# A wait of GpSimd for VectorE's products in a fused recurrence and highway layer, with another list of operations

## The chip, the core and the metric

The kernel runs on one core of a Trainium2 chip. The metric is the device time of one execution in microseconds (us). The engines are named as in the profile: PE is TensorE (PEld its weight loads), DVE is VectorE, ACT is ScalarE, POOL is GpSimd, SP is SyncE, which here issues the transfers. Each engine works through its own queue in order, and they wait for each other by semaphores.

## The reference

Two layers in a row. The first is a gated recurrence over 6,336 steps for 4 sequences of 256 channels, the second a highway layer on its 25,344 outputs:

```
f = lower_bound + (1 - lower_bound) * sigmoid(f_logit)
h = f[:, t] * h + (1 - f[:, t]) * x[:, t]        # for each t; y[:, t] = h
H = max(y @ w_h, 0)
T = sigmoid(y @ w_t + b_t)
out = T * H + (1 - T) * y
```

## The kernel before

The tokens are cut into 29 units, most of 1,024 tokens, the first three and the last three smaller, and one that takes the ends of all four sequences (unit 14). The 256 channels are two halves of 128 partitions. Every unit passes through the same steps, each of which is a small function named by one letter:

- l, x: the loads of f_logit and x, issued by SyncE (w is the store of the output).
- u: on ScalarE, the sigmoid of -f_logit, in f16.
- b: the product of u and x, in pieces of 512 columns, written to bv. Both inputs lie in SBUF. It runs on GpSimd, or on VectorE where the list has a "v" behind it.
- i and p: on TensorE, the transposes of u and of bv, to channels by tokens, into PSUM (tiles uT and bT).
- f: the gate, from uT, on ScalarE (with a "v" on VectorE).
- s: on VectorE, the scan that is the recurrence, from f in SBUF and bT in PSUM, one for each half; it carries the last column on to the next unit.
- z and g: on TensorE, the two matrix products of the highway layer, into PSUM.
- t: on ScalarE, the sigmoid of z.
- d: on VectorE, from y in SBUF and g in PSUM, the maximum and the subtraction of y (the scale 1 - lower_bound is folded into the weights and into the sums).
- E and e: the product of d and t, both in SBUF, which together cover 2 x 1,024 columns of a unit. The last number of each entry of `units` says how many of these columns GpSimd takes, in pieces of 512 (E, with a piece number); VectorE takes the rest in one operation (e). Where the number is 2,048, there is no e; where it is 0, no E.
- o: on TensorE, y times a diagonal plus e, transposed back; c: the copy of the result from PSUM to SBUF, on ScalarE (with "v" on VectorE).

There is no loop over the units: the string `order` lists all these operations one by one, as letter, unit, piece and, behind a colon, the PSUM slot. `pin` keeps the instructions in this order, so the list gives each engine's queue: an engine's queue is the list, cut down to that engine's operations. "e10" is thus VectorE's product of unit 10, and "b15.2" the third bv product of unit 15. Tiles rotate through the numbers of buffers given in `bufs` (6 for l and x, 3 for u and bv, 4 for y, 2 for t, d and e).

The lines in the profile of before: u L233, b L242, i L249, f L264 (VectorE) and L266 (ScalarE), p L280, s L297, z and g L308, t L321, d L326, E and e L332, o L351 and L352, c L360 (VectorE) and L362 (ScalarE).

Of the kernel before, what the change touches and what calls it, by code (L numbers as in the profile page):

```python
# [19 lines left out]
def kernel(  # L20
# [10 lines left out]
    nc = tc.nc  # L31
# [16 lines left out]
        (0, 128, 8, 5120, 'yk', 4, 768),
        (1, 128, 8, 0, 'y', 4, 512),
        (1, 128, 8, 1024, 'y', 4, 2048),  # L50
        (1, 128, 8, 2048, 'y', 4, 1024),
        (1, 128, 8, 3072, 'y', 4, 512),
        (1, 128, 8, 4096, 'y', 4, 0),
        (1, 128, 8, 5120, 'y', 4, 2048),
# [1 line left out]
        (2, 128, 8, 192, 'y', 4, 1024),
        (2, 128, 8, 1216, 'y', 4, 2048),
        (2, 128, 8, 2240, 'y', 4, 768),
        (2, 128, 8, 3264, 'y', 4, 1280),
        (2, 128, 8, 4288, 'y', 4, 2048),  # L60
        (2, 128, 8, 5312, 'y', 4, 1280),
# [1 line left out]
        (3, 128, 8, 1216, 'y', 4, 512),
        (3, 128, 8, 2240, 'y', 4, 2048),
        (3, 128, 8, 3264, 'y', 4, 1024),
        (3, 128, 8, 4288, 'y', 4, 1792),
# [11 lines left out]
c1.0 f4.1 t3.0 s4.0 g3.0:1 i5.0:1 p4.1:0 z3.1:2 d3.0 s4.1 b5.0 b5.2 b5.3 b5.1 f5.0 u6 g3.1:0 t3.1 o2.0:1 E3.0
i5.1:1 p5.0:0 E3.1 d3.1 z4.0:2 s5.0 f5.1 g4.0:0 i6.0:1 p5.1:0 c2.0 u7 t4.0 f6.0 b6.0 d4.0 z4.1:1 g4.1:0 E3.2
b6.2 b6.1 b6.3 s5.1 i6.1:1 e3 d4.1 u8 t4.1 z5.0:2 E4.0 b7.0 p6.0:0 b7.3 t5.0 x8 E4.1 b7.2 f6.1 l10 w0.0 g5.0:0  # L80
l9 z5.1:1 o3.1:2 w2.0 p6.1:1 s6.0 i7.0:0 d5.0 x11 w1.0 b7.1 c3.1 b8.0 x9 b8.2 o3.0:0 b8.1 f7.0 t5.1 c3.0
g5.1:2 s6.1 d5.1 p7.0:0 i8.0:1 e4 f8.0 E5.0 z6.0:1 t6.0 s7.0 E5.1 b8.3 E5.2 x10 g6.0:0 p7.1:1 g6.1:2 i7.1:0
d6.0 z6.1:1 u9 o4.1:0 E5.3 d6.1 o4.0:2 f7.1 u10 b9.0 p8.0:0 c4.0 s7.1 s8.0 i8.1:1 l11 c4.1v t6.1 w3.1 w3.0
z7.0:2 l12 w4.0 f8.1 t7.0 b9.3 b9.1 E6.0 b10.0 x12 g7.0:1 E6.1 i9.0:1 f9.0 i10.1:0 g7.1:2 z7.1:0 b9.2 d7.0
d7.1 f10.1 E6.2 u11 p8.1:1 s8.1 o5.0:1 c5.0 E6.3 o5.1:2 E7.0 c5.1 w5.0 p9.0:0 i9.1:1 t7.1 s9.0 g8.0:1 E7.1
b10.1 d8.0 o6.1:2 p9.1:0 b10.3 l13 w4.1 z8.0:0 w5.1 f9.1 c6.1 i10.0:1 x13 u12 w6.1 l15 b10.2 s9.1 g8.1:1 l14
z8.1:2 e7 p10.0:0 t8.0 d8.1 g9.0:0 t8.1 b11.0 o6.0:2 f10.0 u13 c6.0 d9.0 b11.3 p10.1:1 o7.1:1 z9.0:0 s10.0
c7.1 w6.0 E8.0 b11.1 i11.0:0 g9.1:2 b12.0 z9.1:1 t9.0 s10.1 f11.0 o7.0:0 b12.1 t9.1 d9.1 b11.2 e8 E9.0 w7.1
E9.1 i12.1:1 b12.3 b12.2 p11.0:0 s11.0 f12.1 z10.0:2 c7.0 i11.1:1 g10.0:1 f11.1 x14 d10.0 i12.0:0 p11.1:1
o8.0:0 s11.1 t10.0 w7.0 f12.0 l16 E9.2 c8.0 E9.3 p12.0:0 o8.1:2 u14 x15 s12.0 c8.1 z11.0:1 w8.0 i13.0:1 t11.0  # L90
b13.0 g11.0:0 f13.0 x16 z10.1:2 w8.1 d11.0 p12.1:0 o9.1:1 b13.2 t10.1 b13.1 g11.1:0 l17 b13.3 E10.0 c9.1 w9.1
# [6 lines left out]
p16.0:0 t14.1 i17.1:1 s16.0 o12.1:1 c12.0 x19 f17.1 w12.0 g15.0:2 d14.1 i17.0:0 E13.3 l20 b17.3 c12.1 w12.1
p16.1:1 b18.2 b18.3 d15.0 f17.0 x20 s16.1 z15.0:1 p17.0:0 o13.1:0 u19 o13.0:2 e14 t15.0 E15.0 c13.0 E15.1
i18.0:1 c13.1 s17.0 z15.1:1 z16.0:2 t15.1 t16.0 g15.1:0 d15.1 b19.0 g16.0:1 b18.1 w13.0 d16.0 f18.0 b19.3  # L100
o14.1:2 i19.0:0 p17.1:1 c14.1 f19.0 w13.1 o14.0:0 i18.1:0 l21 u20 b19.2 s17.1 E16.0 b19.1 g16.1:2 d16.1
z16.1:1 p18.0:1 x21 w14.1 l22 z17.0:2 e15 E16.1 f18.1 c14.0 w14.0 x22 b20.0 o15.1:0 p18.1:0 t16.1 t17.0
# [5 lines left out]
p21.0:0 w17.1 z20.1:0 E19.1 u23 c17.0 z20.0:1 p21.1:1 t20.0 b22.3 E19.2 E19.3 w17.0 s21.0 b23.0 b23.3 s21.1
t20.1 x24 o18.0:2 i22.0:0 g20.0:1 l26 g20.1:0 c18.0 d20.0 b23.1 o18.1:2 d20.1 p22.0:1 l25 E20.0 f22.0 u24
o19.1:1 s22.0 z21.0:0 p22.1:0 c18.1 t21.0 g21.0:2 i23.0:1 c19.1 z21.1:0 s22.1 b23.2 E20.1 e20 w18.0 o19.0:1  # L110
f23.0 x25 b24.0 t21.1 E20.2 c19.0 p23.0:1 i23.1:0 d21.0 z22.0:0 g22.0:2 f23.1 s23.0 i24.1:0 t22.0 b24.1 d22.0
E21.0 b24.3 g21.1:1 f24.1 w18.1 x27 d21.1 b24.2 E21.1 u25 z22.1:0 p23.1:1 t22.1 E21.2 x26 i24.0:0 g22.1:2
o20.0:1 s23.1 w19.1 l27 d22.1 o20.1:0 E21.3 b25.0 f24.0 c20.0 b25.1 p24.0:1 i25.1:0 c20.1 s24.0 z23.0:1 u26
b25.3 E22.0 g23.0:2 o21.1:0 d23.0 w19.0 t23.0 p24.1:1 s24.1 f25.1 o21.0:1 w20.0 l28 i25.0:0 E23.0 b25.2
g23.1:2 c21.1 z23.1:0 d23.1 c21.0 x28 w20.1 z24.0:1 e22 p25.0:1 f25.0 u28 t23.1 E23.1 E23.2 t24.0 p25.1:0
z24.1:2 g24.0:0 o22.0:1 t24.1 w21.0 u27 E23.3 s25.0 o22.1:2 d24.0 i26.0:1 c22.0 s25.1 E24.0 f26.0 w21.1
o23.1:0 c22.1 g24.1:1 i26.1:1 b26.0 d24.1 c23.1 i27.0:0 g25.0:2 f27.0 f26.1 z25.0:0 i27.1:0 d25.0 w22.1 w22.0
b26.1 w23.1 p26.0:1 f27.1 z25.1:1 E24.1 e24 b27.0 p26.1:0 s26.0 t25.0 s26.1 b28.0 t25.1 o24.1:2 o23.0:0 c24.1
p27.0:1 s27.0 g25.1:1 c23.0 z26.0:2 i28.1:0 t26.0 o24.0:0 p27.1:1 f28.1 d25.1 E25.0 g26.0:2 e25 s27.1 z26.1:1
w23.0 c24.0 w24.1 d26.0 p28.0:0 E25.1 E25.2 g26.1:0 d26.1 i28.0:1 w24.0 t26.1 e26 z27.0:2 E25.3 t27.0 f28.0  # L120
o25.1:1 g27.0:0 d27.0 o25.0:2 c25.1 z27.1:0 p28.1:1 s28.0 w25.1 o26.0:1 c25.0 g27.1:2 t27.1 s28.1 d27.1
g28.0:0 d28.0 c26.0 e27 z28.0:2 t28.0 g28.1:1 z28.1:0 t28.1 d28.1 e28 o27.0:2 w25.0 c27.0 w26.0 o28.1:1 c28.1
o28.0:0 w27.0 c28.0v w28.1 w28.0
"""

    NU = len(units)
# [109 lines left out]
    def do_b(n, k, eng, slot):  # L236
        np_ = units[n][1]
        if "bv" not in st[n]:
            st[n]["bv"] = sb([P, NB // 2, D, 2], BF16, "bv")
# [2 lines left out]
        pin(e.tensor_mul(st[n]["bv"][:np_, k].rearrange("p d j -> p j d"), st[n]["u"][:np_, q:q + 2],  # L242
                         st[n]["x"][:np_, q:q + 2]))
# [85 lines left out]
    def times(n, eng, a, e):  # L329
        if "e" not in st[n]:  # L330
            st[n]["e"] = flat("e")
        pin(eng.tensor_mul(st[n]["e"][:, a:e], st[n]["d"][:, a:e], st[n]["t"][:, a:e]))  # L332
# [75 lines left out]
```

## Time and profile before

| | us |
|---|---|
| median of 3 runs | 230.56 |
| lowest, highest | 228.42, 241.39 |
| the profiled execution | 228.91 |
| its span | 227.1 |
| DMA: HBM read, written | 52.43 MB, 25.95 MB |

The span goes from the first to the last instruction of the profiled execution. A row of a table of groups gives line, engine and operation, what is written and read with its shape, how often, and then busy time in us, the mean of one in ns, and the idle time of the engine just before them with what ended it. A row of the order of time gives its start in us from the start of the span, how long it took, engine, line and tile, and the count where several were merged; behind it, in brackets, stands idle time before it. A row of waits gives who waited for whom: us in total, how often, and the longest. In a table of stretches each engine has its busy time and, in brackets, its instructions; then come the clock that TensorE was granted (1 is full speed), the share of the DMA engines that was busy, and GB/s.

### The profile page before, as it was taken

The numbers are of one execution on the slowest core, as the hardware profiler recorded it, in microseconds if no ns is written. First come the engines' busy times: TensorE is split into PE (matmuls) and PEld (weight loads), VectorE is DVE, ScalarE is ACT, GpSimd is POOL, SyncE is SP. The second block draws the span as 40 slices with busy tenths as digits, with TensorE's granted clock in tenths as the row PEclk, the third lists the DMA queues.
The fourth block names the chain that finished last, engine by engine and source line by source line (L and its number), as shares of the span: only waits on it lengthen the run. The fifth ranks groups of instructions, "written<-read, shape, count | busy, mean of one in ns | idle before, by whom it ended". The sixth has DMA issues, their size and how long they took to land.

```text
span 227.1 us, 4665 instructions
## 1 busy us (share of the span) xinstructions
PE 189.4 (83%) x1784; PEld 134.3 (59%) x1811; DVE 212.3 (93%) x164; ACT 195.8 (86%) x196; POOL 178.0 (78%) x167
## 2 busy tenths in 40 slices
...
GB/s 187 384 423 421 420 420 418 413 422 421 415 388 318 429 412 419 362 422 428 74 271 382 273 272 416 389 389 351 424 379 331 369 414 266 277 131 270 142 294 223
DMA packets 16751, 78.69 MB, mean 346 GB/s; under 512 B 2004, under 2 KB 2776, under 8 KB 11096
## 3 DMA queue, kind: packets, MB, share of 16 engines
...
q10 hardware_dynamic: 8, 0.00, 0.0%
HBM read 52.43 MB, written 25.95 MB: 345 GB/s over the span
## 4 chain that ended last, share of the span: by engine, by line
PE 31%; DVE 24%; DMA 16%; ACT 11%; POOL 8%; issue 6%; SPq 1%; DVEq 0%; ACTq 0%; POOLq 0%
DMA x<-in_x_dram 10%; DVE y L297 9%; DVE e L332 8%; PE g L308 7%; DMA l<-in_f_logit_dram 7%; PE z L308 6%; DVE d L326 5%; PE op L352 5%; PE op L351 5%; POOL e L332 5%; PE uT L249 4%; ACT f L266 4%; PE bT L280 4%; POOL bv L242 4%; ACT u L233 4%
## 5 line engine op out<-in xcount | busy, mean ns | idle before, releaser
L242 POOL TENSOR_TENSOR bv<-u,x 128x512 bf16<-128x512 f16 x96 | 110.9, 1182 | 14.2 <-ACT u L233 8.7
L297 DVE TENSOR_TENSOR_SCAN y<-f,y,bT 128x1024 bf16<-128x1024 f16 (+2 forms) x46 | 93.1, 2035 | 1.4 <-PE bT L280 1.0
L332 POOL TENSOR_TENSOR e<-d,t 128x512 bf16<-128x512 bf16 (+1 forms) x60 | 68.4, 1153 | 23.5 <-PE op L352 14.7
L321 ACT ACTIVATE t<-z,bt 128x1024 bf16<-128x1024 f32 (+3 forms) x58 | 57.9, 1030 | 13.6 <-DVE e L332 9.0
L308 PEld LDWEIGHTS <-w_sb 128*128 128x128 f16 x416 | 39.8, 100 | 37.8 <-issue 7.9
L266 ACT ACTIVATE f<-uT,ncc 128x1024 f16<-128x1024 f16 (+3 forms) x56 | 58.3, 1048 | 4.3 <-PE uT L249 4.2
L326 DVE SCALAR_TENSOR_TENSOR d<-y,ncc,g 128x1024 bf16<-128x1024 bf16 (+2 forms) x54 | 59.1, 1106 | 2.7 <-PE g L308 2.2
L351 PE MATMUL op<-diag,y 128*128 128x128 f16 x368 | 46.7, 221 | 9.8 <-DVE d L326 9.1
L362 ACT COPY o<-op 128x1024 f32<-128x1024 f32 (+2 forms) x51 | 50.6, 1016 | 4.8 <-PE op L352 4.3
L233 ACT ACTIVATE u<-l 128x2048 f16<-128x2048 f32 (+3 forms) x29 | 49.4, 1705 | 3.7 <-DMA l<-in_f_logit_dram 3.7
L352 PEld LDWEIGHTS <-e 128*128 128x128 bf16 x396 | 44.3, 114 | 14.0 <-issue 11.0
L308 PE MATMUL g<-y,w_sb 128*128 128x512 bf16 (+1 forms) x181 | 47.8, 374 | 5.2 <-DVE d L326 3.7
L352 PE MATMUL op<-ident_b,e 128*128 128x128 bf16 x396 | 50.3, 221 | 0.9 <-DVE e L332 0.9
L308 PE MATMUL z<-y,w_sb 128*128 128x512 bf16 (+1 forms) x178 | 47.9, 376 | 1.4 <-DVE d L326 0.2
L351 PEld LDWEIGHTS <-y 128*128 128x128 bf16 x368 | 41.2, 113 | 2.2
L249 PE MATMUL uT<-ident_h,u 128*128 128x128 f16 x396 | 32.3, 223 | 9.9 <-ACT f L266 4.5
L249 PEld LDWEIGHTS <-u 128*128 128x128 f16 x396 | 27.0, 100 | 18.6 <-issue 9.8
L280 PE MATMUL bT<-ident_f,bv 128*128 128x128 f32 x198 | 32.5, 281 | 5.4 <-DVE y L297 2.7
L332 DVE TENSOR_TENSOR e<-d,t 128x1024 bf16<-128x1024 bf16 (+6 forms) x21 | 31.5, 1500 | 0.6 <-ACT t L321 0.2
L280 PEld LDWEIGHTS bT<-ident_f,bv 128*128 128x128 f32 x198 | 22.7, 143 | 12.3 <-POOL bv L242 3.5
L297 DVE TENSOR_TENSOR_SCAN y<-f,yr,bT 128x1024 bf16<-128x1024 f16 x4 | 9.2, 2328 | 0.0
L297 DVE TENSOR_TENSOR_SCAN y<-f,bT 128x256 bf16<-128x256 f16 (+1 forms) x4 | 5.9, 1468 | 0.0
...
## 6 DMA issues: line engine op xcount, KB each, us to landing
...
```

The costliest lines, as they stand in the source:

```text
L233: pin(nc.scalar.activation(u[:np_, :nb], st[n]["l"][:np_, :nb], AF.Sigmoid, scale=-1.0))
L242: pin(e.tensor_mul(st[n]["bv"][:np_, k].rearrange("p d j -> p j d"), st[n]["u"][:np_, q:q + 2], st[n]["x"][:np_, q:q + 2]))
L249: pin(nc.tensor.transpose(uT[:, j * np_:(j + 1) * np_], st[n]["u"][:np_, j, h * P:(h + 1) * P], ident_h[:np_, :np_]))
L266: pin(nc.scalar.activation(to, of, AF.Identity, scale=ncc[:, h:h + 1], bias=1.0))
L280: pin(nc.tensor.transpose(to, pair, ident_f[:np_, :np_]))
L297: pin(nc.vector.tensor_tensor_scan(y[:, c0:c0 + ln], st[n]["f", h][:, c0:c0 + ln], st[n]["bT", h][:, c0:c0 + ln], 0.0 if prev is None else ...
L308: pin(nc.tensor.matmul(p[:, a:e], w_sb[:, k, ki, m * P:(m + 1) * P], half(n, "y", ki)[:, a:e], start=ki == 0, stop=ki == NH - 1))
L321: pin(nc.scalar.activation(half(n, "t", m), st[n]["z", m][:, :tokens(n)], AF.Sigmoid, bias=bt[:, m:m + 1]))
L326: pin(nc.vector.scalar_tensor_tensor(half(n, "d", m), half(n, "y", m), ncc[:, m:m + 1], st[n]["g", m][:, :tokens(n)], op0=ALU.mult, op1=AL ...
L332: pin(eng.tensor_mul(st[n]["e"][:, a:e], st[n]["d"][:, a:e], st[n]["t"][:, a:e]))
L351: pin(nc.tensor.matmul(o, half(n, "y", h)[:, cols], diag[:, h], start=True, stop=False))
L352: pin(nc.tensor.matmul(o, half(n, "e", h)[:, cols], ident_b, start=False, stop=True))
```

## The change

A helper remembers the last VectorE operation with two SBUF inputs (an e, or a b on VectorE). The first GpSimd operation (b or E) that the list has behind it gets a dependency on it, and so waits until it has ended:

```diff
+    held = []
+
+    def shared(ins, gpsimd):
+
+        if not gpsimd:
+            held[:] = [ins]
+        elif held:
+            tc.add_manual_dep(ins.ins, held.pop().ins.name, mybir.DependencyInfo(
+                mybir.DependencyClass.Sync, mybir.DependencyReason.DATA), reason="shared port")
...
         e = nc.vector if eng else nc.gpsimd
-        pin(e.tensor_mul(st[n]["bv"][:np_, k].rearrange("p d j -> p j d"), st[n]["u"][:np_, q:q + 2],
-                         st[n]["x"][:np_, q:q + 2]))
+        shared(pin(e.tensor_mul(st[n]["bv"][:np_, k].rearrange("p d j -> p j d"), st[n]["u"][:np_, q:q + 2],
+                                st[n]["x"][:np_, q:q + 2])), not eng)
...
-        pin(eng.tensor_mul(st[n]["e"][:, a:e], st[n]["d"][:, a:e], st[n]["t"][:, a:e]))
+        shared(pin(eng.tensor_mul(st[n]["e"][:, a:e], st[n]["d"][:, a:e], st[n]["t"][:, a:e])), eng is nc.gpsimd)
```

The second part is the list. `order` is another string from the first line to the last, and the share of GpSimd in the products of d and t is another in 19 of the 29 units. In all, GpSimd has 95 bv products (96 before) and 60 E with 29,440 columns (60 with 28,928), VectorE 19 e with 21,248 columns (21 with 21,760), 4 bv products (3), 5 f (2) and no output copy (2). 18 GpSimd operations get the new dependency: 15 behind an e, three behind a bv product. Some lines of both lists, among them those around e10 in the old one and e19 in the new one:

```diff
-l0 x0 wh u0 cc i0.1:0 i0.0:1 l1 x1 wt b0.0 l2 dg x2 l3 x3 f0.0 u1 l4 x4 b1.0 WH l5 f0.1 x5 p0.0:1 i1.0:0 s0.0
...
-o9.0:2 p13.0:1 b14.0 x17 u15 s12.1 z11.1:1 i13.1:0 d11.1 c9.0 t11.1 w9.0 E11.0 E10.1 b14.2 f13.1 s13.0 g10.1:0
-d10.1 g12.0:2 i14.1:1 b15.0 f14.1 e10 i14.0:0 p13.1:1 u16 f14.0 z12.0:1 d12.0 t12.0 b15.2 g12.1:0 b14.1
-o10.0:2 s13.1 e11 l18 i15.0:0 c10.0 f15.0 d12.1 z12.1:1 p14.0:1 o10.1:2 b16.0 t12.1 b15.1 b15.3 b16.3 p14.1:0
...
+l0 u0 x0 b0.0v i0.0:0 cc f0.0 x1 p0.0:1 p0.1:0 l1 s0.0 u1 l2 dg wh u2 i0.1:1 f0.1v wt i1.1:1 s0.1 i2.0:0 x2
...
+i15.0:0 f15.0v x16 w9.0 w9.1 o10.1:0 f14.0 p14.0:1 u16 b15.1 b15.2 E12.0 t12.1 g13.0:1 l18 c10.1 s14.0 z13.1:2
...
+o18.0:2 E19.0 c17.0 l27 c18.0 o18.1:0 w17.1 l24 p21.1:1 i22.0:0 z20.0:1 e19 w17.0 s21.1 c18.1 g20.0:2 d20.0
+b22.1 t20.0 E19.1 f22.0 b23.0 g20.1:0 x24 l25 w18.0 d20.1 E20.0 i23.1:1 E20.1 b23.3 z20.1:1 p22.0:0 o19.1:2
+s22.0 z21.0:0 f23.1 p22.1:1 t20.1 c19.1 t21.0 E20.2 u24 x25 w18.1 b23.2 g21.0:1 o19.0:2 g21.1:0 s22.1 d21.0
...
```

More of the change, by code (lines that the diff above doesn't have):

```diff
@@ L44 @@
         (0, 128, 8, 1024, 'y', 4, 1280),
-        (0, 128, 8, 2048, 'y', 4, 768),
-        (0, 128, 8, 3072, 'y', 4, 2048),
+        (0, 128, 8, 2048, 'y', 4, 2048),
+        (0, 128, 8, 3072, 'y', 4, 0),
         (0, 128, 8, 4096, 'y', 4, 2048),
[L48 to L54, printed above, removed]
-        ((0, 1, 2, 3), 128, 6, [6144, 6144, 0, 0], 'yr', 4, 0),
[L56 to L61, printed above, removed]
+        (0, 128, 8, 5120, 'yk', 4, 0),
+        (1, 128, 8, 0, 'y', 4, 2048),
+        (1, 128, 8, 1024, 'y', 4, 1024),
+        (1, 128, 8, 2048, 'y', 4, 768),
+        (1, 128, 8, 3072, 'y', 4, 2048),
+        (1, 128, 8, 4096, 'y', 4, 2048),
+        (1, 128, 8, 5120, 'y', 4, 768),
+        ((0, 1, 2, 3), 128, 6, [6144, 6144, 0, 0], 'yr', 4, 0),
+        (2, 128, 8, 192, 'y', 4, 2048),
+        (2, 128, 8, 1216, 'y', 4, 768),
+        (2, 128, 8, 2240, 'y', 4, 0),
+        (2, 128, 8, 3264, 'y', 4, 2048),
+        (2, 128, 8, 4288, 'y', 4, 1024),
+        (2, 128, 8, 5312, 'y', 4, 1536),
         (3, 128, 8, 192, 'y', 4, 2048),
[L63 to L66, printed above, removed]
+        (3, 128, 8, 1216, 'y', 4, 768),
+        (3, 128, 8, 2240, 'y', 4, 1024),
+        (3, 128, 8, 3264, 'y', 4, 2048),
+        (3, 128, 8, 4288, 'y', 4, 2048),
         (3, 128, 4, 5312, 'y', 4, 0),
@@ L78 @@
[L78 to L91, printed above, removed]
-o9.0:2 p13.0:1 b14.0 x17 u15 s12.1 z11.1:1 i13.1:0 d11.1 c9.0 t11.1 w9.0 E11.0 E10.1 b14.2 f13.1 s13.0 g10.1:0
@@ L98 @@
[L98 to L102, printed above, removed]
@@ L108 @@
[L108 to L112, printed above, removed]
@@ L113 @@
[L113 to L122, printed above, removed]
@@ L123 @@
-o28.0:0 w27.0 c28.0v w28.1 w28.0
+l0 u0 x0 b0.0v i0.0:0 cc f0.0 x1 p0.0:1 p0.1:0 l1 s0.0 u1 l2 dg wh u2 i0.1:1 f0.1v wt i1.1:1 s0.1 i2.0:0 x2
+f2.0 WH f1.1 g0.0:0 i1.0:0 b2.0 b1.0v p1.0:1 b2.1 f1.0 l3 x3 WT z0.0:1 t0.0 d0.0 g0.1:2 z0.1:0 p1.1:0 l4 s1.0
+s1.1 d0.1 p2.0:1 x4 s2.0 l5 t0.1 u3 g1.0:1 i2.1:0 z1.0:0 i3.0:1 b3.0 f2.1v b3.3v p2.1:0 b3.1 x5 t1.0 f3.0 d1.0
+s2.1 z1.1:2 i3.1:1 t1.1 g1.1:0 f3.1 b3.2v p3.0:0 u4 d1.1 e0 b4.0 s3.0 b4.1 z2.0:1 o0.0:2 z2.1:0 t2.0 p3.1:1 l6
+g2.1:1 i4.1:0 s3.1 t2.1 b4.3 c0.0 f4.1 x6 l7 g2.0:0 x7 u5 b4.2 b5.0 d2.0 b5.1 d2.1 i4.0:0 e1 f4.0 e2 g3.0:2
@@ new lines @@
+z3.0:0 d3.0 p4.0:1 i5.1:0 z3.1:1 t3.0 f5.1 b5.2 b5.3 p4.1:0 o1.0:2 l8 E3.0 g3.1:0 u6 s4.0 b6.0 E3.1 c1.0 t3.1
+i5.0:1 s4.1 f5.0 d3.1 o2.0:2 w0.0 b6.2 E3.2 p5.0:0 b6.1 i6.1:1 z4.0:1 g4.0:0 s5.0 d4.0 c2.0 f6.1 t4.0 E4.0
+p5.1:1 i6.0:0 z4.1:2 b6.3 u7 e3 o3.1:1 g4.1:0 s5.1 d4.1 t4.1 f6.0 c3.1 o3.0:2 p6.0:1 u8 l10 x8 c3.0 z5.1:1
+p6.1:0 z5.0:0 b7.0 t5.0 s6.0 s6.1 l9 w3.0 i7.0:1 g5.0:2 b7.1 b7.2 x9 g5.1:0 t5.1 f7.0 i7.1:0 b7.3 p7.0:1 d5.0
+w3.1 E4.1 E4.2 w2.0 f7.1 u9 g6.0:1 b8.0 i8.0:0 b8.3 E4.3 w1.0 b8.2 d5.1 f8.0 s7.0 z6.0:2 t6.0 b9.0 p7.1:1 l11
@@ new lines @@
+i9.0:0 d6.0 g6.1:0 z6.1:2 s7.1 b8.1 u10 f9.0 o4.1:1 b9.1 t6.1 d6.1 i8.1:1 p8.0:0 f8.1 c4.1 e5 x10 z7.0:0
+o4.0:2 s8.0 p8.1:1 c4.0 b9.3 b9.2 E6.0 b10.0 o5.0:1 x11 s8.1 z7.1:2 t7.0 c5.0 p9.0:0 g7.0:0 d7.0 t7.1 i9.1:1
+u11 o5.1:1 E6.1 s9.0 E6.2 z8.0:2 g7.1:0 f9.1 c5.1 b10.1 i10.1:1 d7.1 f10.1 p9.1:0 E6.3 z8.1:1 g8.0:0 i10.0:1
+t8.0 w4.1 s9.1 o6.0:2 t8.1 b11.0 f10.0 d8.0 b10.2 b10.3 o6.1:1 l12 l13 w4.0 E8.0 p10.0:0 c6.0 i11.0:1 x12 w5.0
+w5.1 c6.1 b11.2 b11.1 e7 b11.3 s10.0 g8.1:0 f11.0 d8.1 E8.1 o7.1:2 w6.0 x13 u12 i11.1:1 p10.1:0 l14 b12.0 E8.2
@@ new lines @@
+w6.1 c7.1 x14 z9.0:1 g9.0:0 t9.0 o7.0:2 s10.1 f11.1 w7.1 p11.0:0 c7.0 w7.0 d9.0 E8.3 z9.1:1 g9.1:0 s11.0
+i12.0:1 E9.0 d9.1 b12.2 u13 o8.1:2 l15 p11.1:0 t9.1 b12.1 c8.1 z10.0:1 f12.0 b12.3 t10.0 E9.1 g10.0:0 g10.1:2
+s11.1 u14 p12.0:1 i13.1:0 o8.0:1 d10.0 f13.1 c8.0 d10.1 z10.1:0 b13.0 z11.0:2 i12.1:0 g11.0:1 s12.0 E10.0
+t10.1 b13.3 e9 E10.1 f12.1 i13.0:1 b14.0 z11.1:0 b13.2 t11.0 b13.1 e10 x15 p12.1:0 w8.1 o9.0:2 d11.0 l16 s12.1
+t11.1 g11.1:1 l17 d11.1 w8.0 b14.1 o9.1:0 f13.0 p13.0:1 i14.1:0 c9.0 c9.1 f14.1 z12.0:2 E11.0 E11.1 g12.0:1
@@ new lines @@
+p13.1:0 u15 b14.2 s13.0 t12.0 o10.0:0 b15.0 d12.0 s13.1 i14.0:1 g12.1:1 E11.2 c10.0 d12.1 E11.3 z12.1:2
+i15.0:0 f15.0v x16 w9.0 w9.1 o10.1:0 f14.0 p14.0:1 u16 b15.1 b15.2 E12.0 t12.1 g13.0:1 l18 c10.1 s14.0 z13.1:2
+i15.1:0 u17 d13.0 f15.1 z13.0:0 p14.1:1 s14.1 E12.1 b15.3 b16.0 o11.1:1 p15.0:0 s15.0 b16.1 t13.0 i16.1:1
+g13.1:0 E12.2 c11.1 t13.1 f16.1 o11.0:1 E12.3 g14.0:2 l19 d13.1 d14.0 i16.0:0 u18 p15.1:1 o12.0:0 f16.0
+z14.0:2 b16.2 E13.0 c12.0 w10.0 b16.3 x17 i17.0:0 w10.1 s15.1 e13 E13.1 g14.1:0 x18 c11.0 g15.0:1 b17.0 d14.1
@@ new lines @@
+b17.2 t14.0 f17.0 p16.0:1 z15.0:2 z14.1:0 b17.1 d15.0 s16.0 b18.0 b17.3 u19 o12.1:1 p16.1:0 t14.1 z15.1:0
+w11.1 i18.0:1 w12.0 t15.0 l20 c12.1 b18.1 t15.1 b18.2 o13.0:2 w12.1 g15.1:1 w11.0 o13.1:0 e14 E15.0 x19 E15.1
+f18.0 p17.0:1 s16.1 c13.0 b18.3 l21 d15.1 i17.1:0 s17.0 z16.0:2 c13.1 f17.1 g16.0:1 p17.1:0 i18.1:1 o14.0:0
+t16.0 w13.0 x20 o14.1:2 E15.2 u20 c14.1 c14.0 d16.0 s17.1 g16.1:1 w13.1 f18.1 z16.1:2 E16.0 E15.3 p18.0:0 x21
+d16.1 t16.1 z17.0:0 E16.1 b19.0 b19.3 p18.1:1 b19.2 g17.0:1 s18.0 b19.1 g17.1:2 t17.0 l22 u21 i19.0:0 f19.0
@@ new lines @@
+d17.0 s18.1 w14.1 z17.1:0 t17.1 o15.1:1 e16 i19.1:0 p19.0:1 b20.0 w14.0 x22 b20.1 b20.2 l23 c15.1 f19.1
+o15.0:0 d17.1 z18.0:1 g18.0:2 i20.0:0 c15.0 s19.0 b21.0 b20.3 t18.0 g18.1:0 w15.1 f20.0 d18.0 i20.1:1 d18.1
+z18.1:1 p19.1:0 f20.1 b21.3 b21.2 p20.0:1 o16.0:2 o16.1:0 t18.1 s19.1 u22 E18.0 e17 c16.0 c16.1 s20.0 E18.1
+b21.1 E18.2 b22.0 w15.0 w16.0 E18.3 b22.3 i21.1:0 g19.0:1 z19.0:2 f21.1 t19.0 z19.1:0 t19.1 d19.0 w16.1
+i21.0:0 p20.1:1 f21.0 s20.1 g19.1:2 o17.0:1 b22.2 o17.1:0 u23 x23 p21.0:0 c17.1 d19.1 i22.1:1 f22.1 s21.0
@@ new lines @@
+o18.0:2 E19.0 c17.0 l27 c18.0 o18.1:0 w17.1 l24 p21.1:1 i22.0:0 z20.0:1 e19 w17.0 s21.1 c18.1 g20.0:2 d20.0
+b22.1 t20.0 E19.1 f22.0 b23.0 g20.1:0 x24 l25 w18.0 d20.1 E20.0 i23.1:1 E20.1 b23.3 z20.1:1 p22.0:0 o19.1:2
+s22.0 z21.0:0 f23.1 p22.1:1 t20.1 c19.1 t21.0 E20.2 u24 x25 w18.1 b23.2 g21.0:1 o19.0:2 g21.1:0 s22.1 d21.0
+b23.1 E21.0 b24.0 c19.0 i24.0:0 i23.0:1 b24.3 g22.0:2 z21.1:1 b24.1 f24.0 f23.0 p23.0:0 e20 t21.1 d21.1 d22.0
+b24.2 p23.1:1 u25 s23.0 E21.1 o20.1:0 z22.0:2 g22.1:1 c20.1 t22.0 i25.1:0 o20.0:0 s23.1 f25.1 c20.0 d22.1
```

23 lines of the change are left out of this document (11 added, 12 removed).

## The prediction

> **What bounds the kernel now.** I read four views: the page's first part, a table of the span cut into four stretches, the waits, and the order of time around the one place where that table looks odd. The page and the table:
>
> ```profile
> span 227.1 us, 4665 instructions
> PE 189.4 (83%) x1784; PEld 134.3 (59%) x1811; DVE 212.3 (93%) x164; ACT 195.8 (86%) x196; POOL 178.0 (78%) x167
> ...
> core 0: us, PE busy (x) PEld busy (x) DVE busy (x) ACT busy (x) POOL busy (x), PEclk, DMA share, GB/s
> 24.00:98.70 74.70, 65.50 (x624) 46.13 (x633) 73.88 (x44) 71.92 (x65) 70.75 (x63) 1.00 1.01 404
> 98.70:119.50 20.80, 11.22 (x94) 8.00 (x93) 20.24 (x14) 10.69 (x10) 10.10 (x10) 0.75 0.74 286
> 119.50:216.30 96.80, 90.84 (x902) 65.43 (x914) 95.39 (x63) 92.16 (x93) 87.07 (x77) 1.00 0.85 322
> 216.30:227.10 10.80, 6.21 (x80) 5.00 (x78) 5.63 (x11) 6.05 (x10) 0.00 (x0) 0.98 0.66 253
> ```
>
> VectorE (DVE) sets the pace: it works in 73.88 of the 74.70 us of the first of these stretches, 20.24 of 20.80 in the second and 95.39 of 96.80 in the third. ScalarE (ACT) and GpSimd (POOL) are close behind in the first and third, with 71.92 and 92.16, and 70.75 and 87.07 us. The second stretch is the odd one: VectorE is as busy as ever, and the other engines work half of the time. What they wait for there, and what VectorE does:
>
> ```profile
> POOL e L332 <- PE op L352: 14.7, 2, 14.1
> ACT t L321 <- DVE e L332: 9.0, 4, 7.6
> PE op L351 <- DVE d L326: 9.1, 1, 9.1
> ...
> 98.76 10.58 DVE L332 TENSOR_TENSOR e<-d,t 128x1024 bf16<-128x1024 bf16 x1
> 112.93 0.93 DVE L332 TENSOR_TENSOR e<-d,t 128x1536 bf16<-128x1536 bf16 x1
> 120.53 1.22 DVE L332 TENSOR_TENSOR e<-d,t 128x2048 bf16<-128x2048 bf16 x1
> ...
> 97.59 11.21 POOL L242 TENSOR_TENSOR bv<-u,x 128x512 bf16<-128x512 f16 x10
> ```
>
> A product of 1,024 columns (e10 of the list) takes 10.58 us on VectorE, and a little later one of 2,048 columns takes 1.22. The long one begins at 98.76 while GpSimd runs ten bv products without a gap, from 97.59 to 108.80; it ends at 109.34, that is 0.54 us after the last of them. So I read it this way: the two engines cannot read two SBUF operands side by side, GpSimd keeps the right of way as long as its next operation is ready, and e10 did its work when GpSimd had run dry. ScalarE and TensorE stood behind it for 7.6 and 9.1 us, and GpSimd, which had run ahead, then idled for 14.1.
>
> [...]
>
> **What the waiting costs today.** The products on VectorE by size, and those which show the waiting:
>
> ```profile
> L332 DVE TENSOR_TENSOR e<-d,t 128x1024 bf16<-128x1024 bf16 x5 | 14.2, 2849 | 0.2
> L332 DVE TENSOR_TENSOR e<-d,t 128x768 bf16<-128x768 bf16 x3 | 5.6, 1871 | 0.0
> L332 DVE TENSOR_TENSOR e<-d,t 128x1536 bf16<-128x1536 bf16 x4 | 4.3, 1078 | 0.0
> L332 DVE TENSOR_TENSOR e<-d,t 128x1280 bf16<-128x1280 bf16 x3 | 4.2, 1387 | 0.0
> L332 DVE TENSOR_TENSOR e<-d,t 128x512 bf16<-128x512 bf16 x4 | 1.7, 416 | 0.2 <-ACT t L321 0.2
> ...
> 26.41 0.67 DVE L332 TENSOR_TENSOR e<-d,t 128x1024 bf16<-128x1024 bf16 x1
> 39.93 1.54 DVE L332 TENSOR_TENSOR e<-d,t 128x768 bf16<-128x768 bf16 x1
> 49.48 1.07 DVE L332 TENSOR_TENSOR e<-d,t 128x1280 bf16<-128x1280 bf16 x1
> 70.89 2.20 DVE L332 TENSOR_TENSOR e<-d,t 128x1280 bf16<-128x1280 bf16 x1
> 179.50 3.27 DVE L332 TENSOR_TENSOR e<-d,t 128x768 bf16<-128x768 bf16 x1
> 198.79 1.50 DVE L332 TENSOR_TENSOR e<-d,t 128x1536 bf16<-128x1536 bf16 x1
> 208.46 1.62 DVE L332 TENSOR_TENSOR e<-d,t 128x1024 bf16<-128x1024 bf16 x1
> ...
> 48.72 2.85 POOL L332 TENSOR_TENSOR e<-d,t 128x512 bf16<-128x512 bf16 x2
> ```
>
> Undisturbed, the sizes lie on a line: 0.41 us for 512 columns, 0.67 for 1,024, 0.93 for 1,536, 1.22 for 2,048. Between them I estimate 0.54 for 768 and 0.80 for 1,280. Against these the excess is, in the first stretch, 1.54 - 0.54 = 1.00 (e3), 0.27 (e4) and 1.40 (e7), together 2.7 us; in the second, 10.58 - 0.67 = 9.9; in the third, 3.27 - 0.54 = 2.73 (e20), 0.57 (e22) and 0.95 (e24), together 4.2. The GpSimd row shows the other half of the exclusion: its two operations took 2.85 us instead of 2.24, since e4 came between them.
>
> **The change, part by part.** *The wait.* The first GpSimd operation listed behind each e (and each bv product on VectorE) now starts when that product has ended, so nothing listed later can starve it. GpSimd operations listed earlier still can. I take each stretch by itself, because what a shorter VectorE is worth is capped by the next engine there. First: 2.7 of excess goes, and ScalarE's 71.92 allows 74.70 - 71.92 = 2.8, so 2.7. Second: VectorE falls to 20.24 - 9.9 = 10.3 and ScalarE's 10.69 and TensorE's 11.22 are next; I take 20.8 to 11.2, so 9.6. (TensorE's 11.22 is at a granted clock of 0.75, where the stretches on both sides show 1.00; that may go too, and is left out.) Third: 4.2, and ScalarE's 92.16 allows 96.80 - 92.16 = 4.6. Together 16.5 us: 227.1 to 210.6.
>
> *What stays of the lock.* Of the 19 e in the new list, 16 have GpSimd work listed around them. Each may still find an operation in progress which is listed earlier: between nothing (GpSimd already stands at the wait) and 1.12 us. e4 met the end of one and lost 0.27. I take 0.3 each: 16 x 0.3 = 5 us; the bounds are 0 and 18.
>
> *What GpSimd pays.* Behind the waiting operation its whole queue stands, bv and E alike, and after them TensorE's transposes of bv, and the scans. Its work between 24 and 216.3 us is 70.75 + 10.10 + 87.07 = 167.9 us. The new list gives it nearly the same work (95 bv instead of 96, 60 E with 512 columns more). To it come the products for which it stands still, 12.2 us by the clean prices (three of 512 columns, one of 768, four of 1,024, four of 1,280, one of 1,536, three of 2,048), and a handover for 18 waits (15 behind an e, three behind a bv product). The trace of before has none from VectorE to GpSimd; the nearest is ScalarE's start behind e10:
>
> ```profile
> 109.46 1.11 ACT L321 ACTIVATE t<-z,bt 128x1024 bf16<-128x1024 f32 x1 [7.63 <-DVE e L332]
> ```
>
> which is 0.12 us after 109.34, so some 2 us. About 3 us of such standing (0.6 of it in the row of 48.72) are in the 167.9 already. That makes 167.9 + 12.2 + 2.2 - 3 = 179.3 us of the 192.3 between those points, which would themselves shrink to 192.3 - 16.5 + 5 = 180.8. GpSimd would thus be occupied 99%, where it was 70.75 / 74.70 = 95% in the first stretch, and some of its idle time (for data, for ScalarE) will remain. I add 1 us for it; the bounds are 0 and, at 95%, 179.3 / 0.95 = 188.7 - 180.8 = 8.
>
> What covers the standing: in the new list the tightest place is e19, with bv 22.1 held behind it. Between e19 and the scan s22.0 that needs it VectorE has one scan and two d, while GpSimd needs one bv:
>
> ```profile
> L297 DVE TENSOR_TENSOR_SCAN y<-f,y,bT 128x1024 bf16<-128x1024 f16 x36 | 83.9, 2337 | 1.1 <-PE bT L280 0.7 <-PE op L352 0.3
> L326 DVE SCALAR_TENSOR_TENSOR d<-y,ncc,g 128x1024 bf16<-128x1024 bf16 x42 | 52.6, 1263 | 0.9 <-PE g L308 0.6
> L264 DVE TENSOR_SCALAR f<-uT,ncc 128x512 f16<-128x512 f16 x1 | 0.7, 746 | 0.0
> L264 DVE TENSOR_SCALAR f<-uT,ncc 128x256 f16<-128x256 f16 x1 | 0.5, 453 | 0.0
> L360 DVE COPY o<-op 128x1024 f32<-128x1024 f32 x1 | 1.2, 1191 | 0.0
> L360 DVE COPY o<-op 128x256 f32<-128x256 f32 x1 | 0.4, 425 | 0.7 <-PE op L352 0.7
> L242 DVE TENSOR_TENSOR bv<-u,x 128x512 bf16<-128x512 f16 x3 | 1.9, 710 | 0.0
> ...
> POOL bv L242 <- DMA x<-in_x_dram: 5.5, 2, 3.4
> ACT u L233 <- DMA l<-in_f_logit_dram: 3.7, 4, 1.7
> ```
>
> 2.34 + 2 x 1.26 = 4.9 us of cover against 1.12 and the transposes: over 3 us of slack. If that cover were gone, each us that GpSimd comes later would be one on VectorE.
>
> *Operations that move to and from VectorE.* To it: f of 1,024 columns (f15.0, an estimate of 1.33 by the two f rows) and, net, two of 256 (0.9), and one bv product (0.71). From it: the two output copies (1.19 and 0.43), and 0.5 of e (13.7 us of clean products instead of 14.2). Net +0.8 us on VectorE, and about as much off ScalarE.
>
> *The rest of the list* only reorders the same kinds of work, SyncE's queue of 58 loads and 53 stores included. Waiting for loads costs 5.5 + 3.7 us in all; a better or worse order of transfers could move at most about that, either way, and I see no reason for a sign: 0.
>
> **The sum.** 227.1 - 16.5 + 5 + 1 + 0.8 = 217.4 us of span. The profiled execution's own time is 228.91, 1.8 above its span, and just under the median of the three runs, 230.56 (they spread from 228.42 to 241.39, so today's luck with the lock differs from run to run). Forecast: 217.4 + 1.8, about 219 us.
>
> **Rivals.** *GpSimd becomes the bound.* For it: the 99% above. Against: before the long e10 it ran ten operations ahead without need and then idled for 14.1 us, so it has time to give. With 8 us instead of 1: 219 + 7 = 226.
>
> *The long product was no starvation.* Suppose that an e waits for one operation of GpSimd at most, 1.12 us. Then e10's 10.58 us had another cause, the wait has nothing to remove, the meetings of up to 1.12 us stay on both sides, and the time stays where it is, near 229. Against it: e10 ends half a us after the tenth operation, which leaves about a clean length of 0.67 for its work, and e20 lost 2.73 us and e7 1.40, both more than one operation. [...]
>
> *Slower: GpSimd falls behind its list.* The wait protects e from later operations alone. If GpSimd, held 18 times, is late by whole operations, then each e comes upon a backlog that is listed earlier, and waits for all of it, with GpSimd's right of way as above. Place: every e from e3 on. Price: 1.12 us for each operation of backlog at each of 16 e, so 18 us for one and 36 for two. One operation gives 219 + 18 = 237; from a backlog of about one operation at each e this decides the sign. For it: GpSimd's 99%. Against: the slack of 3 us in the tightest place, and that at e10 in the old list GpSimd was ahead, not behind.
>
> **Chances.** Forecast (214 to 222): 0.55. GpSimd bound (222 to 226): 0.15. Nothing gained (226 to 232): 0.13. Slower: 0.12. Better than 214, when nothing of the lock remains (219 - 5): 0.05. The range from 213 to 231 leaves out the slower rival and a little on both sides. A measurement of this kernel can tell about 2% from no change, which is 226 and 235 around the median of 230.56. Faster by more than that: 0.55 + 0.15 + 0.05, less a little of the GpSimd case, 0.74; within it 0.15; slower 0.11.
>
> **What would show it.** In the changed kernel's trace, no e above its clean length by more than about 1.1 us, and the sum of e on VectorE near 13.7 + 5 instead of 31.5 (that is 14.2 + 5.6 + 4.3 + 4.2 + 1.7 and 1.5 in two single ones); a new wait of GpSimd for VectorE's e, some 10 us in all; no stretch in which ScalarE and TensorE stand together; ScalarE and GpSimd at or above 90% of the span. The forecast is wrong if VectorE shows idle time in front of its scans (bv came late), or if e is long behind operations that are listed earlier.

## The result and the profile after

The changed kernel takes 217.43 us (median of 4 runs, 216.98 to 219.43), the kernel before 230.91 (4 runs). The ratio is 0.947, with a 95% interval from 0.938 to 0.955: 5.3% faster, where 219 us was forecast. Here and below a median is of all executions, and a ratio leaves out those more than 1.5% above the fastest of the same kernel. From the page of the changed kernel, and its table of the span in stretches (engine, busy time, instructions; then clock, DMA share, GB/s):

```profile
span 215.2 us, 4648 instructions
PE 190.1 (88%) x1784; PEld 132.4 (62%) x1811; DVE 199.2 (93%) x164; ACT 195.9 (91%) x195; POOL 178.9 (83%) x166
...
L342 DVE TENSOR_TENSOR e<-d,t 128x512 bf16<-128x512 bf16 (+5 forms) x19 | 17.7, 943 | 1.0 <-PE op L362 0.7
```

```profile
0.00:24.00 24.00, 16.70 (x96) 9.08 (x98) 17.77 (x33) 15.83 (x21) 9.46 (x18) 1.00 0.94 361
24.00:98.70 74.70, 67.46 (x631) 47.04 (x642) 72.82 (x48) 72.08 (x66) 69.85 (x61) 1.00 1.01 397
98.70:119.50 20.80, 19.33 (x185) 13.41 (x187) 20.17 (x20) 20.80 (x20) 20.04 (x20) 1.00 1.02 421
119.50:204.10 84.60, 81.13 (x813) 58.55 (x822) 84.55 (x58) 81.47 (x82) 78.51 (x70) 1.00 0.89 342
```

The account closes on VectorE. Its busy time falls from 212.3 to 199.2 us, 13.1 less; its idle time rises from 227.1 - 212.3 = 14.8 to 16.0. The difference, 11.9 us, is the difference of the spans. The e alone fall from 31.5 to 17.7, 13.8 us; everything else on VectorE gains 0.7. The rise of the idle time lies at the end: VectorE's last operation ends at 223.74 of 227.1 us before and at 210.55 of 215.2 after, so 1.2 us more come behind it (the last output copy, which VectorE made before, is now ScalarE's). The waits between its operations add up to the same, 11.5 us before and 11.4 after.

The stretch from 98.70 to 119.50, in which three engines stood half the time, now has all of them at 19.3 us or more of 20.8, with TensorE's clock at 1.00 instead of 0.75. (These are the same microseconds, and with the other list not quite the same operations.)

What is left of the lock (the name used here for the time that e and GpSimd's operations, all with two SBUF inputs, lose beside each other; e10 took 10.58 us for a clean 0.67), in the order of time around e7, VectorE first, then GpSimd, and the new waits in the list of waits (total, times, longest):

```profile
70.86 2.29 DVE L342 TENSOR_TENSOR e<-d,t 128x2048 bf16<-128x2048 bf16 x1 [0.71 <-PE op L362]
...
70.91 1.16 POOL L342 TENSOR_TENSOR e<-d,t 128x512 bf16<-128x512 bf16 x1
72.02 3.30 POOL L252 TENSOR_TENSOR bv<-u,x 128x512 bf16<-128x512 f16 x2
```

```profile
POOL bv L252 <- DVE w_sb L197: 9.0, 1, 9.0
...
POOL e L342 <- DVE e L342: 3.0, 3, 1.2
...
POOL bv L252 <- DVE e L342: 2.2, 2, 1.5
```

e7 has 2,048 columns, a clean 1.22 us. It lost 1.07: GpSimd's E8.0, listed ahead of it, began 0.05 us after it and went first; then e7 got in, and the next bv (b11.2, also listed ahead) stretched: two took 3.30 instead of 2.24 (one is 1.12 us, the 11.21 of the row of ten before, divided by ten). No e lost more than this. GpSimd's own standing for the products shows as 3.0 + 2.2 = 5.2 us.

### The profile page after: what moved, and what is told of

Same layout as the page of the kernel before. It is cut to its first block, busy times and chain, and to the rows that moved or that the text cites. A ratio compares the mean times of both kernels' runs of the same rounds, so it can differ in the third digit from the quotient of the medians.

```text
span 215.2 us, 4648 instructions
## 1 busy us (share of the span) xinstructions
PE 190.1 (88%) x1784; PEld 132.4 (62%) x1811; DVE 199.2 (93%) x164; ACT 195.9 (91%) x195; POOL 178.9 (83%) x166
## 5 line engine op out<-in xcount | busy, mean ns | idle before, releaser
L252 POOL TENSOR_TENSOR bv<-u,x 128x512 bf16<-128x512 f16 x95 | 112.8, 1217 | 21.7 <-DVE w_sb L197 9.0
L342 POOL TENSOR_TENSOR e<-d,t 128x512 bf16<-128x512 bf16 (+1 forms) x60 | 67.7, 1148 | 3.9 <-DVE e L342 3.0
L276 ACT ACTIVATE f<-uT,ncc 128x1024 f16<-128x1024 f16 (+3 forms) x53 | 55.4, 1057 | 4.2 <-PE uT L259 2.8
L318 PEld LDWEIGHTS <-w_sb 128*128 128x128 f16 x416 | 39.3, 99 | 32.2 <-issue 2.7
L372 ACT COPY o<-op 128x1024 f32<-128x1024 f32 (+2 forms) x53 | 51.2, 983 | 4.7 <-PE op L362 3.1
L362 PE MATMUL op<-ident_b,e 128*128 128x128 bf16 x396 | 49.4, 219 | 1.0 <-DVE e L342 0.8
L361 PE MATMUL op<-diag,y 128*128 128x128 f16 x368 | 45.9, 219 | 1.6 <-ACT o L372 0.9
L290 PE MATMUL bT<-ident_f,bv 128*128 128x128 f32 x198 | 33.6, 283 | 7.2 <-POOL bv L252 2.5
L342 DVE TENSOR_TENSOR e<-d,t 128x512 bf16<-128x512 bf16 (+5 forms) x19 | 17.7, 943 | 1.0 <-PE op L362 0.7
L252 DVE TENSOR_TENSOR bv<-u,x 128x512 bf16<-128x512 f16 x4 | 3.4, 855 | 3.1 <-DMA x<-in_x_dram 3.1
## 6 DMA issues: line engine op xcount, KB each, us to landing
x<-in_x_dram SPq DMA_DIRECT2D x22, 1024.0 KB, 13.8
```

Of the source, the lines that this page charges most:

```text
L252: shared(pin(e.tensor_mul(st[n]["bv"][:np_, k].rearrange("p d j -> p j d"), st[n]["u"][:np_, q:q + 2], st[n]["x"][:np_, q:q + 2])), not eng)
L276: pin(nc.scalar.activation(to, of, AF.Identity, scale=ncc[:, h:h + 1], bias=1.0))
L290: pin(nc.tensor.transpose(to, pair, ident_f[:np_, :np_]))
L318: pin(nc.tensor.matmul(p[:, a:e], w_sb[:, k, ki, m * P:(m + 1) * P], half(n, "y", ki)[:, a:e], start=ki == 0, stop=ki == NH - 1))
L342: shared(pin(eng.tensor_mul(st[n]["e"][:, a:e], st[n]["d"][:, a:e], st[n]["t"][:, a:e])), eng is nc.gpsimd)
L361: pin(nc.tensor.matmul(o, half(n, "y", h)[:, cols], diag[:, h], start=True, stop=False))
```

## The experiments

Two questions: is it the wait or the list, and is it true that GpSimd keeps the right of way? Kernels that ran together share their runs of the kernel before, and are compared with those; that kernel had medians of 233.69 and 232.66 us there.

**The wait on the old list.** The old units and the old list, with the helper of the change as it stands (some lines, against the changed kernel):

```diff
-        (0, 128, 8, 2048, 'y', 4, 2048),
-        (0, 128, 8, 3072, 'y', 4, 0),
+        (0, 128, 8, 2048, 'y', 4, 768),
+        (0, 128, 8, 3072, 'y', 4, 2048),
...
-l0 u0 x0 b0.0v i0.0:0 cc f0.0 x1 p0.0:1 p0.1:0 l1 s0.0 u1 l2 dg wh u2 i0.1:1 f0.1v wt i1.1:1 s0.1 i2.0:0 x2
+l0 x0 wh u0 cc i0.1:0 i0.0:1 l1 x1 wt b0.0 l2 dg x2 l3 x3 f0.0 u1 l4 x4 b1.0 WH l5 f0.1 x5 p0.0:1 i1.0:0 s0.0
...
```

> The old list with the wait behind every product of two SBUF inputs on VectorE. Theory (the wait removes the starvation, and that is the gain): e10 takes at most 0.67 + 2 x 1.12 = 2.9 us (b14.2 and b15.0 are listed ahead of it) instead of 10.58, the sum of e on VectorE falls from 31.5 to below 20, and the time to about 219 (217 to 222). Rival (the new list makes the gain): the sum of e falls, but another engine ends later in its place, and the time stays at 226 or more.

218.92 us, ratio 0.941 (0.932 to 0.950). The sum of e is 19.5 us, and e10 took 1.94. Order of time, VectorE, then GpSimd:

```profile
97.56 1.94 DVE L342 TENSOR_TENSOR e<-d,t 128x1024 bf16<-128x1024 bf16 x1
...
96.64 2.31 POOL L252 TENSOR_TENSOR bv<-u,x 128x512 bf16<-128x512 f16 x2
99.57 2.30 POOL L252 TENSOR_TENSOR bv<-u,x 128x512 bf16<-128x512 f16 x2 [0.62 <-DVE e L342]
```

e10 waits for the two bv listed ahead of it, b14.2 and b15.0; then e10 runs while GpSimd stands. The wait alone brings the bulk of the gain.

**The new list without the wait.** The changed kernel without the helper, so with the new units and list, and its products as they were before:

```diff
-        shared(pin(eng.tensor_mul(st[n]["e"][:, a:e], st[n]["d"][:, a:e], st[n]["t"][:, a:e])), eng is nc.gpsimd)
+        pin(eng.tensor_mul(st[n]["e"][:, a:e], st[n]["d"][:, a:e], st[n]["t"][:, a:e]))
```

> The new list without the wait. Theory (wait alone): VectorE's products starve again wherever GpSimd has two or more ready operations; the sum of e is 22 us or more instead of 17.7, with single ones over 3 us, and the time 220 to 230. Rival (list alone): the sum of e stays near 18 and the time at 216 to 218.5.

233.34 us, ratio 0.989 (0.978 to 1.000), longer than either side expected. Its profiled execution took 239.22, the longest of four; in it the sum of e is 38.4 us:

```profile
37.82 8.64 DVE L332 TENSOR_TENSOR e<-d,t 128x768 bf16<-128x768 bf16 x1
...
124.95 8.68 DVE L332 TENSOR_TENSOR e<-d,t 128x1280 bf16<-128x1280 bf16 x1
...
38.22 1.14 POOL L332 TENSOR_TENSOR e<-d,t 128x512 bf16<-128x512 bf16 x1
39.33 5.60 POOL L242 TENSOR_TENSOR bv<-u,x 128x512 bf16<-128x512 f16 x5
44.90 1.14 POOL L332 TENSOR_TENSOR e<-d,t 128x512 bf16<-128x512 bf16 x1
```

The picture of e10 again, at other places: e3 and e13 take 8.6 and 8.7 us while GpSimd works through seven operations behind the one it was at, and e3 ends at 46.46, 0.42 after the last. (e20 takes 5.4.) A gain by the list alone isn't clear of noise: the medians lie 0.35 us apart, and the interval of the ratio reaches 1.000. The rival that credits the list alone falls.

**One wait alone.** The old list, a wait only behind e10:

```diff
     def do_e(n, k, eng, slot):
         times(n, nc.vector, units[n][6], NH * tokens(n))
+        if n != 10:
+            held.clear()
```

(The three behind bv products are off as well.)

> The old list with one single wait: b15.2 behind e10. Theory: e10 falls from 10.58 to at most 2.9 us, the other products keep their lengths on the whole, and some 8 of the 13.5 us come back: 220 to 224. Rival (the long product only moves): another e with a backlog of bv behind it (e11, whose followers are b16.0, b15.1, b15.3, b16.3) takes over 5 us, and the time is 226 or more.

225.44 us, ratio 0.960 (0.949 to 0.971): between the two expectations, 224 and 226; of its four executions two lie in the theory's range (223.46 and 223.97 us) and two in the rival's (226.90 and 230.58). e10 falls to 1.65, and e11 does not take its place:

```profile
99.89 1.65 DVE L344 TENSOR_TENSOR e<-d,t 128x1024 bf16<-128x1024 bf16 x1
105.12 1.86 DVE L344 TENSOR_TENSOR e<-d,t 128x1536 bf16<-128x1536 bf16 x1
...
151.70 3.14 DVE L344 TENSOR_TENSOR e<-d,t 128x1280 bf16<-128x1280 bf16 x1
...
173.45 3.26 DVE L344 TENSOR_TENSOR e<-d,t 128x768 bf16<-128x768 bf16 x1
```

e20 at 173.45 is as long as in the kernel before (3.27), and e17 at 151.70, which took 0.89 there, now took 3.14. So the expectation that the others keep their lengths holds for e20 and not for e17. One wait removes one long product; which of the others is late differs between two executions.

**The first three waits.** The new list with the 15 waits behind e only:

```diff
+        if gpsimd is None:
+            return
         if not gpsimd:
             held[:] = [ins]
...
-                                st[n]["x"][:np_, q:q + 2])), not eng)
+                                st[n]["x"][:np_, q:q + 2])), True if not eng else None)
```

> The new list with the 15 waits behind an e, without the three behind a bv product on VectorE in the first 20 us (one of which held GpSimd for 9.0 us). Theory (the start is set by the loads, the standing is covered): the same time as the change, within 1 us. Rival (GpSimd's 9 us at the start are lost to the end, since it has little idle time): 1 to 4 us faster than the change.

217.96 us, ratio 0.933 (0.922 to 0.943), beside 218.92 of the old list with the wait in the same runs. The change itself was not among them. Its 217.43 us is within the 1 us that the theory allows; but the ratio here, 0.933, is below the change's 0.947, so the times alone don't settle it. GpSimd's first product here:

```profile
11.40 2.29 POOL L254 TENSOR_TENSOR bv<-u,x 128x512 bf16<-128x512 f16 x2 [9.16 <-ACT f L278]
```

It began at 11.40 us, after 9.16 us of idle time (11.27 and 9.02 in the change), released by ScalarE's f. The gap of 9 us at the start, which the list of waits of the change puts down to VectorE, is therefore not the price of the new wait.

**The list beside the wait.** The change and the old list with the wait, on one chip:

> The changed kernel again, to stand beside the next one on one chip. Theory (the wait makes the gain, the list next to nothing): within 1% of the old list with the wait. Rival (the list was made for the wait): 2% or more faster than the old list with the wait.

> The old list with all waits, again, beside the changed kernel on the same chip: by the theory within 1% of it (217 to 220), by the rival 221 or more.

216.59 us against 221.36; ratios 0.946 (0.939 to 0.953) and 0.963 (0.956 to 0.971). The expectation of 1% fails on this chip: with the wait there, the new list is worth another 4.8 us, 2%, and none of the six executions of one overlaps with those of the other in time. On the chip of the first runs it was 1.0 us (217.96, without the three first waits, against 218.92), inside the spread of four executions each. So the rest of the list is worth something between 1 and 5 us, and the wait alone is the larger part on both chips (232.66 to 221.36 on this one). The waits, the change first, then the old list with the wait:

```profile
POOL bv L252 <- DMA x<-in_x_dram: 5.3, 5, 2.2
POOL bv L252 <- DVE e L342: 3.4, 3, 1.5
...
POOL e L342 <- DVE e L342: 3.0, 3, 1.2
```

```profile
POOL bv L252 <- DMA x<-in_x_dram: 9.0, 4, 3.0
POOL e L342 <- DVE e L342: 8.6, 9, 1.4
...
POOL bv L252 <- DVE e L342: 3.2, 2, 2.6
```

In the old list GpSimd stands 11.8 us behind e, in the new one 6.4, with sums of e of 19.3 and 18.4. On VectorE the difference is idle time: between 24 and 204 us it works 175.9 us in the old list and 178.2 in the new one, and in all nearly the same (200.2 and 199.8). That the new list places e where GpSimd need not stand long would fit; no run separated this from its other differences.

**One operation may pass.** The new list, the wait on the second GpSimd operation behind each product:

```diff
-            held[:] = [ins]
+            held[:] = [ins, ins]
+        elif len(held) == 2:
+            held.pop()
         elif held:
```

> The new list; the wait stands on the second GpSimd operation behind each product, not on the first, so one operation may pass it. Theory (each operation that passes costs VectorE up to 1.12 us where GpSimd is ahead): the sum of e rises from 17.7 by 4 to 12 us and the time to 220 to 228. Rival (the product gets in at the first gap, and only a long backlog starves it): the sum of e rises by less than 3 us and the time stays within 1.5 us of the change.

217.09 us, ratio 0.945 (0.938 to 0.952): the same as the change beside it, and the sum of e is 18.8 against 18.4. The rival holds. One operation more that could pass mostly does not (in the trace it does at two of the 19 e): the product gets in before it. This contradicts the right of way as a rule.

**No operation in progress.** In the new list, for 14 e, the GpSimd operation just ahead of the e goes behind it, as here for e7:

```diff
-b11.1 e7
+e7 b11.1
```

> The new list, with the GpSimd operation just ahead of an e moved to just behind it (14 of the 19 e), so that it waits too and the product meets no operation in progress. Theory (what is left of the lock still costs the time): the sum of e falls from 17.7 to 14 to 15 and the time by 1 to 3 us. Rival (GpSimd has no time to give): the sum of e falls, GpSimd stands longer, and the time is the same or up to 4 us longer.

219.56 us, ratio 0.959 (0.951 to 0.967), 1.4% slower than the change beside it. In its profiled execution (223.05 us, the longest of its runs) the sum of e did not fall either:

```profile
L341 DVE TENSOR_TENSOR e<-d,t 128x512 bf16<-128x512 bf16 (+5 forms) x19 | 19.4, 1033 | 0.7 <-PE op L361 0.5
...
POOL bv L251 <- DVE e L341: 11.2, 6, 2.7
...
POOL e L341 <- DVE e L341: 4.5, 2, 3.8
```

GpSimd stands 15.7 us instead of 6.4, comes later, and the e then meet others of its operations (e7 took 3.44 us, 2.2 more than clean). So the 4 us that the lock still costs were not to be had by holding GpSimd in this way.

**The lock by itself.** What decides whether a product gets in? Four kernels, three with nothing but the two engines and one with other traffic, measured it. A scene is one product of VectorE beside a few GpSimd operations that are ready:

> Not the reference's computation: 36 small scenes. In each GpSimd gets six operations at once (bv products, products of d and t, or both in turn, 512 columns, all ready), and VectorE first does one or two operations with one SBUF and one PSUM input, and then a product of 512 or 1,024 columns with two SBUF inputs. Theory (GpSimd keeps the right of way while its next operation is ready): in most scenes the product ends only after the last of the six, 3 to 6 us long. Rival (one instruction holds the lock, then the other engine is served): the product never waits for more than one operation, at most 1.12 us and its own 0.41 or 0.67. The operations with one PSUM input are as long beside GpSimd as without it, by both.

> Not the reference's computation: 64 scenes of six ready bv products of GpSimd beside one product of 1,024 columns on VectorE, nothing else on the chip. VectorE's operation ahead of it grows by 16 columns from scene to scene, so that the product arrives at another moment of GpSimd's 1.11 us cycle each time. Theory (whether a product gets in is a matter of its arrival within the cycle): it gets in at the first gap in most scenes, and in some it passes over two or more gaps, up to all six. Rival (two engines alone never starve; it takes other traffic): it gets in at the first gap in all 64.

> The same 64 scenes, not the reference's computation either, with 2 MB of loads, six ScalarE operations and six matmuls beside each. Theory (arrival alone): the same scenes as without that traffic, on the whole. Rival (other traffic): the product is starved over two or more operations here and never without it.

> Not the reference's computation. GpSimd has 100 products without a wait between them (bv of 512 columns, products of d and t of 512 and of 256, drawn at random), three times over; beside them VectorE does 36, 24 and 20 products of 768 to 1,536 columns, between which stand operations with one PSUM input (first part), these and a scan (second), and these and two operations that write the product's own input (third). Theory (a long unbroken run of GpSimd, mixed operations, or what stands in front of the product brings the starvation): some products pass over two or more whole operations after the one that they meet, as e10 did. Rival (the lock is passed on after each operation, at most one late): none takes longer than its clean length and 1.25 us, in any of the three parts.

The lengths of the products in the four, in this order (ns: least, median, most):

```profile
L94 DVE TENSOR_TENSOR e<-d,t x36: 483/1019/1547, 9.1 to 252.4; 128x512 bf16<-128x512 bf16 x18, 128x1024 bf16<-128x1024 bf16 x18
```

```profile
L98 DVE TENSOR_TENSOR e<-d,t x64: 683/964/1727, 9.2 to 457.6; 128x1024 bf16<-128x1024 bf16 x64
```

```profile
L98 DVE TENSOR_TENSOR e<-d,t x64: 683/969/1735, 9.2 to 458.7; 128x1024 bf16<-128x1024 bf16 x64
```

```profile
L123 DVE TENSOR_TENSOR e<-d,t x80: 561/1192/13252, 12.5 to 362.3; 128x1024 bf16<-128x1024 bf16 x25, 128x1280 bf16<-128x1280 bf16 x24, 128x768 bf16<-128x768 bf16 x17, 128x1536 bf16<-128x1536 bf16 x14
```

In the first three no product was starved: 1.73 us at most, a clean 0.68 and one operation. A d, with one input in PSUM, shows no such loss: in the kernel before, one of 1,024 columns took 1.26 us beside GpSimd (at 97.40) and one 1.28 while GpSimd stood (at 109.47). Two neighbouring scenes of the second kernel show where the edge lies:

```profile
263.79 0.68 DVE L98 TENSOR_TENSOR e<-d,t 128x1024 bf16<-128x1024 bf16 x1
...
271.00 1.73 DVE L98 TENSOR_TENSOR e<-d,t 128x1024 bf16<-128x1024 bf16 x1
```

The first arrived 1.07 us after the start of an operation of 1.16 and got in when that ended. The second arrived 0.02 later in the cycle and waited for one operation more. In the third kernel loads, ScalarE and TensorE beside them change nothing: 1.73 us at most there too. So in the scenes there is no right of way, and other traffic of this kind doesn't bring it. But the fourth kernel has one product among 80 that behaves like e10:

```profile
259.14 13.25 DVE L123 TENSOR_TENSOR e<-d,t 128x768 bf16<-128x768 bf16 x1
...
257.93 4.52 POOL L71 TENSOR_TENSOR bv<-u,xt 128x512 bf16<-128x512 f16 x4
...
269.08 2.28 POOL L71 TENSOR_TENSOR bv<-u,xt 128x512 bf16<-128x512 f16 x2
271.31 0.67 POOL L96 TENSOR_TENSOR h<-d,t 128x256 bf16<-128x256 bf16 x1
272.06 1.35 POOL L75 TENSOR_TENSOR h<-d,t 128x512 bf16<-128x512 bf16 x1
```

It waited 12.7 us over eleven operations behind the one that it met, and got in behind the first one of 256 columns: there GpSimd's next operation began 0.08 us after the end of the last (271.31 + 0.67 = 271.98, and 272.06), where the rows of operations of 512 columns overlap (269.08 + 2.28 = 271.36, and 271.31). So the two engines alone can do it, rarely (1 of the 80), and this product, once passed over, went on losing for eleven operations. (This one lies in the third part, where the operations just ahead of a product write its input; one case does not show that this matters.) The seven products of the full kernels that two or more operations passed agree with this (e10 and e20 before; e3, e13 and e20 of the new list without the wait; e17 and e20 of the run with one wait): none got in where two rows of GpSimd overlap. e17, at 151.70, did so in a gap of 0.39 us; behind the others GpSimd had nothing for over a microsecond:

```profile
151.87 2.29 POOL L344 TENSOR_TENSOR e<-d,t 128x512 bf16<-128x512 bf16 x2
154.54 0.82 POOL L344 TENSOR_TENSOR e<-d,t 128x256 bf16<-128x256 bf16 x1 [0.39 <-ACT t L333]
```

Which moment starts it stays open: 1 of the 244 products of the four kernels was passed over by two or more operations behind the one that it met, against e10 and e20 among the 21 e of the kernel before. The gap that ended this one was not tried by itself.

## Why the prediction was right

**The terms of the sum.** The span was forecast as 217.4 and is 215.2. The sum of e was to be 13.7 + 5 = 18.7 and is 17.7: what stays of the lock is 4 us. The operations moved to and from VectorE other than e were to add 1.3 and added 0.7. The excess taken out was put at 16.5, after leaving out small cases and capping one stretch by TensorE; the groups hold 31.5 - 14.2 = 17.3. GpSimd's 1 us stands against 1.2 us more idle time on VectorE; but that is the longer end behind VectorE's last operation, and its waits did not grow, so GpSimd cost it nothing that shows. Together 1.0 + 0.6 + 0.8 - 0.2 = 2.2 us, all of the difference (as it must be, since busy and idle time make up the span).

That it comes out so close is in part luck. By these terms the wait alone gives 227.1 - 16.5 + 5 + 1 = 216.6 us of span; the profiled executions of the old list with the wait had 217.2 and 218.0. The list's own gain, put at 0, would make up for that.

**That the long product was starvation** holds: with a wait, e10 fell from 10.58 to 1.94 (the bound was 2.9) and, with this wait alone, to 1.65, and without waits others took its place. The cap by stretches was not put to the test: it took no more than 0.3 us off the sum, and the middle stretch, where ScalarE now works 20.80 of 20.80 us, holds other work than before.

**"GpSimd keeps the right of way as long as its next operation is ready"** was wrong as a rule. In 243 of the 244 products of the last four kernels VectorE got in behind the operation that it met, or behind one more; six of these began 0.00 to 0.02 us ahead of GpSimd's next operation by the rows, and still waited for it. The one left is that of 13.25 us. For the eight products that two or more operations passed, the prediction's sentence does describe what followed: they got in only where GpSimd had nothing ready or left a gap. The forecast of the time did not hang on this: the wait takes away what could starve the product, whatever its chance of being starved (the longest e with it is 2.29 us in the change and 1.94 in the old list). But it made the third rival's price too high, since a backlog mostly costs one operation or less and not all.

**GpSimd as the bound** did not come. Of the stretch from 24 to 204.1 us, GpSimd is busy for 69.85 + 20.04 + 78.51 = 168.4 of 180.1, 94%, and stands 5.2 behind e: 96%, where 99% was worked out. The charge for standing was too high (5.2 seen as idle time behind e, where 12 + 2 were put in and some 10 were to be seen), and the "90% of the span" for GpSimd was wrong (83%).

**The rest of the list at 0** was too low a gain. On one chip it is worth 4.8 us when the wait is there, on another 1.0; without the wait nothing clear of noise.
